# Softmax over slots by two pairs of chunks in the first batch, with a newly searched order of all work

## The chip, the cores and the metric

One core of one Trainium2 chip runs the whole kernel. The metric is device time in microseconds (us), the median of several executions. The engines are TensorE (PE in the rows; its weight loads are PEld), VectorE (DVE), ScalarE (ACT), GpSimd (POOL) and SyncE (SP), whose queue issues nearly all transfers.

## The reference

`x` is 4 batches of 12800 rows of 128 channels; `inducing` is 32 slots of 128. Attention runs twice, then a gated convolution of 5 taps:

```python
def mab(q, kv):
    s = scale * (q @ kv.transpose(0, 2, 1))
    s = s - s.max(-1, keepdims=True)
    a = np.exp(s)
    a /= a.sum(-1, keepdims=True) + 1e-09
    return a @ kv
h = mab(I, x)
x = mab(x, h)
...
for k in range(K):
    gate_pre += conv_w[k][None, None, :] * xp[:, k:k + S, :]
gate = 1.0 / (1.0 + np.exp(-gate_pre))
val = x @ w_val
return (gate * val @ w_out)
```

So the first attention reads all rows of a batch into 32 slots (h), and the second gives each row a softmax over those 32 slots.

## The kernel before

A batch's 12800 rows are four strips of 3200, one for each quarter of the partitions, and the strips are cut into seven chunks of 320 to 480 columns (`SIZES`). In the first batch the order of chunks starts with 1; chunk 0 is last.

For each batch there are two passes. In the first, `s1` (L313) multiplies a chunk of x with the inducing rows; `e1` (L318, VectorE) takes the scores from PSUM and keeps a maximum; `group` makes the negated maximum (L350, L352) on GpSimd or VectorE; `exp1` takes exponentials (L360) and transposes them (L363); `hsum` (L377) sums exp times x into H, which VectorE adds up (L389 to L393). In the first batch most of the transposed x is made by TensorE (L287) and copied out of PSUM (L293 on ScalarE, L295 on VectorE) and not loaded. `prep` turns H into the slots hT (L413, then L420 to L422) and into the convolution's weights W (L481, L490) from `w_val`, `w_out` and `conv_w`, which come as 64-bit numbers in one load (L163) and are converted by VectorE (L176 to L181), then by GpSimd (L192 to L201) or VectorE (L189 to L198); `wts` (L208 to L210) takes three small statistics of them. The slots need `wts` only for what follows them.

In the second pass `s2` (L530) scores a chunk against the slots, `tin` (L534, VectorE) transposes the scores out of PSUM into a tile e, and `joint` does the softmax for a list of chunks at once: maximum (L544, VectorE), subtraction (L549, GpSimd), exponential (L555, ScalarE), sum and reciprocal (L561, L563, L564, VectorE), product (L572, GpSimd), transpose back (L575, VectorE), the high half in f16 (L578, ScalarE) and the low half (L580, GpSimd). `JOINT` lists which chunks go together. A `visit` is the convolution of a chunk (L597 for the gate, L604 for the value); it needs the halves of its own chunk and of the one before. Then come tanh (L695, ScalarE), gate times value (L705, VectorE), two f16 halves (L712 ScalarE, L715 GpSimd), the output product (L786, TensorE), its copy out of PSUM (L798 VectorE or L800 ScalarE) and the store (L804).

Every engine works through its own queue in order. What stands in it is set by three tables: `ORDER` is the order in which all operations are issued, `SLOTS` gives each tile its buffer (PSUM has eight banks, and a product waits until the bank's last reader is done), and `ENGINES` chooses between two engines where an operation allows it. Transfers go in SyncE's queue in the same order.

Of the kernel before, what the change touches and what calls it, by code (L numbers as in the profile page):

```python
# [42 lines left out]
JOINT = [[[0], [1], [2], [3], [4], [5, 6]]] + [[[0], [1, 2], [3, 4], [5, 6]]] * 3  # L43
# [820 lines left out]
def run_plan(tc, plan, slot):  # L864
# [109 lines left out]
]  # L974
ENGINES = [
# [3 lines left out]
]  # L979
# [54 lines left out]
```

## Time and profile before

| | us |
|---|---|
| median of 3 runs | 269.8 (269.4 to 270.52) |
| the profiled execution | 270.69 |
| its span in the profile | 268.6 |
| TensorE busy | 261.0 (97%) |
| VectorE busy | 216.3 (81%) |
| GpSimd busy | 206.1 (77%) |
| ScalarE busy | 195.3 (73%) |

Busy times are shares of the span. TensorE's matmuls are pipelined, so a busy TensorE can hold short stalls that don't show as idle time. The profiled execution lies 0.9 us above the median.

### The profile page before, as it was taken

What the parts mean: (1) busy time and instruction counts of PE and PEld (TensorE: products, weight loads), DVE (VectorE), ACT (ScalarE), POOL (GpSimd) and SP (SyncE); (2) the same over time, 40 slices, a digit from 0 to 9 for tenths busy, and PEclk for the clock granted to TensorE, in tenths of its full rate; (3) what the DMA queues carried; (4) which work ended last, traced back from release to release, by engine and by line L of the source; (5) the groups of instructions that cost most, each with busy time, mean ns of one, the idle gap of its engine ahead of it and who ended that gap; (6) DMA issues with size and microseconds to landing.
All of it is one profiled execution on the core that took longest, in us unless ns stands there. A gap on an engine that the chain in (4) does not pass through costs nothing.

```text
span 268.6 us, 10638 instructions
## 1 busy us (share of the span) xinstructions
PE 261.0 (97%) x4609; PEld 142.1 (53%) x4609; DVE 216.3 (81%) x431; ACT 195.3 (73%) x247; POOL 206.1 (77%) x191
## 2 busy tenths in 40 slices
PE   8999899999999999999999999999999999999994
PEld 4658444476444457464444456457545655444442
DVE  0698799999888998979997888967899897783623
ACT  2466147896667788758778796897679898689674
POOL 1225277798979698886998888988889979989650
PEclk9999999999999999999999999999999999999999
DMA  7999999959999398999869999931550313634486
GB/s 264 424 418 420 414 420 385 355 201 418 343 418 380 115 333 296 357 335 367 316 228 361 350 301 311 399 139 53 198 205 4 142 68 144 223 144 155 156 302 226
DMA packets 22943, 74.48 MB, mean 277 GB/s; under 512 B 1905, under 2 KB 16241, under 8 KB 22897
## 3 DMA queue, kind: packets, MB, share of 16 engines
q1 hardware_dynamic: 22608, 73.61, 72.9%
q8 instruction: 36, 0.59, 0.9%
q10 hardware_dynamic: 288, 0.20, 0.2%
q14 instruction: 11, 0.08, 0.1%
HBM read 47.58 MB, written 26.21 MB: 275 GB/s over the span
## 4 chain that ended last, share of the span: by engine, by line
PE 82%; DMA 7%; DVE 6%; issue 2%; POOL 2%; ACT 1%; DVEq 0%; ACTq 0%
PE banks L597 31%; PE banks L786 23%; PE banks L377 8%; PE banks L530 7%; DMA os<-in_xt_dram 5%; PE banks L604 5%; PE banks L313 4%; DMA indT<-in_indT_dram 1%; PE banks L287 1%; PE banks L741 1%; DVE os L798 1%; PE banks L481 1%; DVE ss L318 1%; DVE z L561 1%; DVE m L544 1%
## 5 line engine op out<-in xcount | busy, mean ns | idle before, releaser
L715 POOL TENSOR_TENSOR gl<-tg,gh 128x960 f16<-128x960 f32 (+2 forms) x54 | 104.6, 1948 | 9.8 <-ACT gh L712 4.2
L597 PE MATMUL banks<-P,W 32*128 32x480 f16 (+3 forms) x1680 | 103.3, 351 | 0.3 <-POOL P L580 0.2
L705 DVE SCALAR_TENSOR_TENSOR tg<-tg,banks 128x960 f32<-128x960 f32 (+4 forms) x57 | 61.4, 1081 | 22.4 <-ACT tg L695 18.9
L597 PEld LDWEIGHTS <-W 32*128 32x128 f16 x1680 | 51.2, 92 | 45.4 <-issue 14.3
L695 ACT ACTIVATE tg<-banks,gsc 128x960 f32<-128x960 f32 (+4 forms) x57 | 55.0, 1007 | 15.8 <-PE banks L597 15.5
L712 ACT CAST gh<-tg 128x960 f16<-128x960 f32 (+2 forms) x54 | 51.5, 960 | 18.3 <-DVE tg L705 10.3
L786 PE MATMUL banks<-gh,wo 128*32 128x480 f16 (+4 forms) x636 | 64.1, 358 | 0.6 <-issue 0.6
L786 PEld LDWEIGHTS <-wo 128*32 128x32 f16 (+1 forms) x954 | 36.0, 97 | 34.9 <-issue 13.7
L786 PE MATMUL banks<-gl,wo 128*32 128x480 f16 (+4 forms) x318 | 43.5, 357 | 0.0
L604 PE MATMUL banks<-P,W 32*128 32x480 f16 (+3 forms) x336 | 41.4, 353 | 0.3 <-DVE ss L318 0.3
L800 ACT ACTIVATE os<-banks,osc 128x960 f32<-128x960 f32 (+2 forms) x33 | 33.8, 1031 | 8.1 <-PE banks L786 8.1
L580 POOL TENSOR_TENSOR P<-pt,P 128x480 f16<-128x480 f32 (+4 forms) x18 | 28.1, 1558 | 3.2 <-ACT P L578 3.0
L572 POOL TENSOR_TENSOR e<-e,z 128x480 f32<-128x480 f32 (+4 forms) x18 | 25.2, 1400 | 6.0 <-DVE z L564 5.5
L377 PE MATMUL banks<-xk,et 128*32 128x129 f32 x800 | 29.5, 275 | 0.2 <-ACT tg L695 0.2
L549 POOL TENSOR_TENSOR e<-e,m 128x480 f32<-128x480 f32 (+4 forms) x18 | 25.1, 1398 | 4.2 <-DVE m L544 4.1
L377 PEld LDWEIGHTS banks<-xk,et 128*32 128x32 f32 x800 | 24.6, 109 | 6.4 <-issue 2.1
L798 DVE TENSOR_SCALAR os<-banks,osc 128x960 f32<-128x960 f32 (+2 forms) x21 | 24.4, 1171 | 2.7 <-PE banks L786 2.6
L530 PE MATMUL banks<-xt,hT 128*32 128x480 f32 (+2 forms) x208 | 25.5, 557 | 0.0
L313 PE MATMUL banks<-xt,indT 128*32 128x480 f32 (+2 forms) x208 | 24.3, 554 | 0.0
L360 ACT ACTIVATE ss<-ss,ng 128x480 f32<-128x480 f32 (+3 forms) x28 | 17.3, 668 | 4.8 <-POOL ng L352 2.5
L534 DVE STREAM_TRANSPOSE e<-banks 128x480 f32<-128x480 f32 (+2 forms) x28 | 18.1, 654 | 1.2 <-PE banks L530 0.5
L363 DVE STREAM_TRANSPOSE et<-ss 128x480 f32<-128x480 f32 (+3 forms) x28 | 17.2, 636 | 1.7 <-ACT ss L360 1.7
(104 smaller groups left out, 263.2 us busy)
## 6 DMA issues: line engine op xcount, KB each, us to landing
xt<-in_xt_dram SPq DMA_DIRECT2D x16, 960.0 KB, 8.6
out_dram<-os SPq DMA_DIRECT2D x30, 480.0 KB, 4.4
xk<-in_xk_dram SPq DMA_DIRECT2D x11, 904.0 KB, 9.2
out_dram<-os SPq DMA_DIRECT2D x22, 448.0 KB, 3.9
xk<-in_xk_dram SPq DMA_DIRECT2D x10, 968.0 KB, 7.9
xt<-in_xt_dram SPq DMA_DIRECT2D x8, 896.0 KB, 11.9
os<-in_xt_dram SPq DMA_DIRECT2D x1, 960.0 KB, 14.6
xk<-in_xk_dram SPq DMA_DIRECT2D x1, 712.0 KB, 9.2
```

Of the source, the lines that this page charges most:

```text
L313: T.matmul(buf(key)[32 * r:32 * r + 32, :n], c_["indT"], x[:, :, r, :], start=True, stop=True)
L377: T.matmul(buf(key)[32 * s:32 * s + 32, :P + 1], buf(("et", b, c))[:, 32 * i:32 * i + 32], buf(("xk", b, c))[:, i, :], start=j < R, stop=j ...
L530: T.matmul(buf(key)[32 * r:32 * r + 32, :n], buf(("hT", b)), x[:, :, r, :], start=True, stop=True)
L580: lambda: G.tensor_tensor(c_["P2"][:, o:o + n], buf(qk)[:, :n], c_["P1"][:, o:o + n], ALU.subtract), ("lo", n),
L597: T.matmul(buf(("ps2", "g", b, c, r // 2))[:, r % 2, :n], buf(("W", b))[q, w, k, :], c_[("P1", "P2")[e]][q, o:o + n], start=u == 0, stop=u ...
L604: T.matmul(buf(("ps2", "v", b, c, r // 2))[:, r % 2, :n], buf(("W", b))[q, w, TAPS, :], c_[("P1", "P2")[e]][q, o:o + n], start=u == 0, sto ...
L695: lambda s=s: S.activation(buf(tg)[:, s, :n], buf(g)[:, s, :n], AF.Tanh, scale=small[b]["gsc"]),
L705: V.scalar_tensor_tensor(t, t, 1.0, buf(v)[:, s, :n], ALU.add, ALU.mult)
L712: op(("hi", b, c, p), "ACT", lambda: S.copy(buf(g1)[:, :, :n], buf(tg)[:, :, :n]), ("act", 2 * n), [("gv", b, c, p, 0)], [g1], [tg])
L715: ENG[e].tensor_tensor(buf(g2)[:, :, :n], buf(tg)[:, :, :n], buf(g1)[:, :, :n], ALU.subtract)
L786: T.matmul(t[s], w[:, s], x, start=j == 0, stop=j == len(terms) - 1)
L800: S.activation(o, a, AF.Copy, scale=small[b]["osc"])
```

## The change

In the first batch the softmax over slots was done for chunks 1, 2, 3 and 4 alone and for 5 with 6. Now it is done for 1 alone, 2 with 3, 4 with 5, and 6 alone. There is one softmax group fewer, 1178 operations in place of 1186. The three tables are new throughout, for all batches.

```diff
-JOINT = [[[0], [1], [2], [3], [4], [5, 6]]] + [[[0], [1, 2], [3, 4], [5, 6]]] * 3
+JOINT = [[[0], [1], [2, 3], [4, 5], [6]]] + [[[0], [1, 2], [3, 4], [5, 6]]] * 3
...
 ORDER = [
-    1, 0, 2, 15, 13, 16, 17, 18, 19, 3, 20, 21, 14, 28, 27, 47, 123, 125, 30, 29, 129, 55, 126, 31, 124, 132,
+    1, 0, 2, 15, 13, 16, 17, 18, 19, 20, 21, 14, 3, 28, 27, 47, 124, 123, 55, 29, 126, 125, 30, 56, 130, 129,
```

First place: SyncE's queue at the start of the program. xt and os are chunks of x, tg is the tile that takes the weights (w), xk a chunk of transposed x.

```order
 L257 DMA xt_64<-in_xt_dram 128x1920
 L257 DMA xt_65<-in_xt_dram 128x1920
-L163 DMA tg_83<-in_w_dram 128x261
 L257 DMA xt_66<-in_xt_dram 128x1920
 L257 DMA os<-in_xt_dram 128x1920
 L257 DMA os<-in_xt_dram 128x1408
+L163 DMA tg_83<-in_w_dram 128x261
 L257 DMA xk_114<-in_xk_dram 128x1936
```

The load of the weights went behind the three loads of chunks 5, 6 and 0.

Second place: VectorE before the slots hT, in the program before. ss and et are a chunk's scores and their transposed exponentials, H the sum, w the converted weights, cmax and wrow what `wts` makes.

```order
L363 STREAM_TRANSPOSE et1_78<-ss4_76 128x480
L335 TENSOR_REDUCE m10_130<-mx0_129 128x1
L363 STREAM_TRANSPOSE et2_79<-ss0_72 128x480
L295 COPY xk0_113<-banks_61 128x7x128
L208 TENSOR_REDUCE cmax_127<-w_123 128x1
L209 TENSOR_SCALAR cmax_127<-cmax_127 128x1
L210 TENSOR_REDUCE wrow_128<-w_123 128x1
L363 STREAM_TRANSPOSE et0_77<-ss1_73 128x320
L391 SCALAR_TENSOR_TENSOR H0_94<-H0_94,f0_133,banks_61 128x129 x2
L420 TENSOR_SCALAR zz0_134<-banks_61 128x32
```

The same stretch of VectorE's queue in the changed program, from the sixth maximum of the batch on:

```order
L335 TENSOR_REDUCE m10_130<-mx0_129 128x1
L176 TENSOR_SCALAR tg1_84<-tg0_83 128x261
L177 SCALAR_TENSOR_TENSOR tg1_84<-tg0_83,tg1_84 128x261
L391 SCALAR_TENSOR_TENSOR H0_94<-H0_94,f0_133,banks_61 128x129
L178 SCALAR_TENSOR_TENSOR tg1_84<-tg0_83,tg1_84 128x261
L318 TENSOR_SCALAR ss1_73,mx0_129<-banks_61 128x320
L179 TENSOR_SCALAR tg1_84<-tg1_84 128x261
...
L189 SCALAR_TENSOR_TENSOR tg2_85<-tg2_85,tg1_84 128x261
L190 TENSOR_TENSOR tg2_85<-tg2_85,tg1_84 128x261
L181 TENSOR_SCALAR tg0_83<-tg0_83 128x261
L391 SCALAR_TENSOR_TENSOR H0_94<-H0_94,f0_133,banks_61 128x129
L198 SCALAR_TENSOR_TENSOR w_123<-tg0_83,tg2_85 128x261
```

The whole conversion now stands among the last steps to H; its last three instructions (L189, L190, L198) were on GpSimd before, and its first (L176) stood some 15 rows further up.

Third place: TensorE's queue from the slots to the first convolution, before. os holds chunks 0 and 6 of the first batch, xt0 to xt4 chunks 1 to 5, xt5 to xt9 chunks of the second batch. The lines left out make W (L481).

```order
L530 MATMUL banks_61<-os_117,hT0_111 32x352 x4
L451 MATMUL banks_61<-hT0_111,w_123 32x32 x4
L530 MATMUL banks_61<-xt0_62,hT0_111 32x480 x4
L530 MATMUL banks_61<-xt2_64,hT0_111 32x480 x4
...
L313 MATMUL banks_61<-xt7_69,indT_121 32x480 x4
L313 MATMUL banks_61<-xt8_70,indT_121 32x448 x4
L313 MATMUL banks_61<-xt9_71,indT_121 32x448 x4
L313 MATMUL banks_61<-xt6_68,indT_121 32x448 x4
```

And in the changed program:

```order
L530 MATMUL banks_61<-os_117,hT0_111 32x352 x4
L451 MATMUL banks_61<-hT0_111,w_123 32x32 x4
L530 MATMUL banks_61<-xt0_62,hT0_111 32x480 x4
L530 MATMUL banks_61<-os_117,hT0_111 32x480 x4
L313 MATMUL banks_61<-xt7_69,indT_121 32x448 x4
...
L313 MATMUL banks_61<-xt5_67,indT_121 32x448 x4
L530 MATMUL banks_61<-xt2_64,hT0_111 32x480 x4
L530 MATMUL banks_61<-xt1_63,hT0_111 32x480 x4
L313 MATMUL banks_61<-xt8_70,indT_121 32x448 x4
...
L530 MATMUL banks_61<-xt3_65,hT0_111 32x480 x4
```

Six slot-score products (L530) stand ahead of the first convolution where three stood, and three scores of the second batch (L313) where four stood.

## Rows read from the trace of the kernel before

**Rows 1.** Stretches: us, busy us of each engine (x instructions), clock, DMA, GB/s

```profile
21.20:30.10 8.90, 8.26 (x169) 6.09 (x158) 6.61 (x22) 4.29 (x8) 3.19 (x9) 1.00 1.01 418
30.10:37.50 7.40, 6.79 (x116) 2.27 (x117) 6.99 (x27) 3.20 (x6) 4.80 (x10) 1.00 1.02 419
37.50:51.20 13.70, 13.04 (x253) 6.76 (x253) 13.38 (x37) 8.22 (x14) 10.86 (x18) 1.00 0.98 380
...
63.80:100.00 36.20, 36.13 (x656) 16.95 (x656) 32.48 (x59) 27.68 (x34) 31.95 (x26) 1.00 0.89 329
100.00:150.00 50.00, 50.00 (x973) 27.53 (x966) 43.62 (x93) 38.31 (x49) 42.87 (x35) 1.00 0.90 322
150.00:200.00 50.00, 49.43 (x1035) 27.97 (x1027) 41.72 (x78) 39.36 (x50) 43.34 (x35) 1.00 0.68 244
...
sum 268.60, PE 261.04 PEld 142.05 DVE 216.29 ACT 195.30 POOL 206.14; mean PE 26.10 PEld 14.21 DVE 21.63 ACT 19.53 POOL 20.61
```

**Rows 2.** Timeline of TensorE: start, us, line, [idle before <-releaser]

```profile
14.29 1.93 PE L377 MATMUL banks<-xk,et 128*32 128x129 f32 x60
...
28.88 0.33 PE L413 MATMUL banks<-pick,H 128*32 128x32 f32 x16 [0.51 <-DVE H L391]
...
30.14 0.80 PE L530 MATMUL banks<-os,hT 128*32 128x352 f32 x8 [0.18 <-DVE hT L422]
...
30.82 1.80 PE L530 MATMUL banks<-xt,hT 128*32 128x480 f32 x16
...
37.48 1.54 PE L597 MATMUL banks<-P,W 32*128 32x320 f16 x40
39.27 0.86 PE L597 MATMUL banks<-P,W 32*128 32x320 f16 x18 [0.24 <-POOL P L580]
...
63.82 0.37 PE L597 MATMUL banks<-P,W 32*128 32x480 f16 x2
...
67.81 0.96 PE L530 MATMUL banks<-xt,hT 128*32 128x448 f32 x8
68.58 0.59 PE L786 MATMUL banks<-gh,wo 128*32 128x480 f16 x8
...
69.19 0.59 PE L786 MATMUL banks<-gh,wo 128*32 128x480 f16 x8
```

**Rows 3.** Groups by line and shape, to 75 us: count, busy us, mean ns

```profile
L575 DVE STREAM_TRANSPOSE pt<-e 128x480 f32<-128x480 f32 x4 | 2.7, 672 | 0.0
...
L544 DVE TENSOR_REDUCE m<-e 128x15 f32<-128x480 f32 x4 | 2.5, 632 | 0.0
...
L575 DVE STREAM_TRANSPOSE pt<-e 128x960 f32<-128x960 f32 x1 | 1.2, 1172 | 0.0
...
L544 DVE TENSOR_REDUCE m<-e 128x30 f32<-128x960 f32 x1 | 1.1, 1146 | 0.0
```

**Rows 4.** Timeline of SyncE's queue, then transfers: KB each, us to landing

```profile
3.15 0.45 SPq L163 DMA_DIRECT2D tg<-in_w_dram  x1
...
4.71 0.81 SPq L257 DMA_DIRECT2D os<-in_xt_dram  x2
...
os<-in_xt_dram SPq DMA_DIRECT2D x1, 704.0 KB, 16.0
...
tg<-in_w_dram SPq DMA_DIRECT2D x1, 261.0 KB, 10.1
```

**Rows 5.** Timeline of VectorE, 15 to 31 us: start, us

```profile
15.22 0.29 DVE L176 TENSOR_SCALAR tg<-tg 128x261 int32<-128x261 int32 x1
...
15.55 0.43 DVE L177 SCALAR_TENSOR_TENSOR tg<-tg,tg 128x261 int32<-128x261 int32 x1
...
21.58 0.85 DVE L352 TENSOR_SCALAR ng<-n 32x1 f32<-32x1 f32 x4
...
29.28 0.19 DVE L420 TENSOR_SCALAR zz<-banks 128x32 f32<-128x32 f32 x1 [0.46 <-PE banks L413]
...
29.90 0.19 DVE L422 TENSOR_TENSOR hT<-banks,zz 128x32 f32<-128x32 f32 x1
```

158 rows, old and new, of tables (ENGINES, ORDER, SLOTS) are left out of this document.

## The prediction

> **What bounds the kernel now.** I read a table of stretches, then TensorE's timeline. In the table [rows 1] the reader is to see two regimes. From 63.8 us on TensorE is busy for 36.13 of 36.20 us and 50.00 of 50.00, at a granted clock of 1.00, and over the whole span for 261.04 of 268.60: there nothing can be won but TensorE's own work. That work does not change. Both programs have 32 runs of convolution matmuls with 33 runs of other matmuls between them, and the same products in sum; the after has a few more output products in one piece and fewer in strips, at the same number of columns.
>
> What is left to decide is the first 64 us, where TensorE has waits and VectorE is nearly full: 6.61 of 8.90 us before the slots hT exist, then 6.99 of 7.40 and 13.38 of 13.70 [rows 1]. In TensorE's timeline [rows 2] the landmarks are: the H matmuls at 28.88 after 0.51 idle, the first slot scores (L530) at 30.14, the first convolution at 37.48, and the convolution of chunk 3, the fourth visit, at 63.82. I measure the change by how much TensorE has done when it reaches that last landmark.
>
> **The pairing itself.** Four single chunks and a pair become two singles and two pairs: 1 and 6 alone, 2 with 3, 4 with 5. That is one softmax group fewer, and with it five VectorE, three GpSimd and two ScalarE instructions fewer. On VectorE two maxima of 480 cost 2 x 0.632 us and one of 960 costs 1.146; two transposes cost 2 x 0.672 against 1.172 [rows 3]. That saves 0.118 and 0.172; the sum, the scaling and the reciprocal, which I take at 0.12 each, make it 0.65 us of VectorE. It is worth 0 if TensorE has other work meanwhile, and 0.65 if VectorE is what TensorE waits for. Against it stands latency: chunk 2 now waits for chunk 3 in every step, each longer by some 0.5 us (1.146 - 0.632).
>
> By the rows the part that an instruction costs whatever its width is 2 x 0.632 - 1.146 = 0.118 us. [...]
>
> **The weights' conversion, moved.** On SyncE's queue the load of the weights (tg from w) went from before the load of chunk 5 to behind the last x load of the batch. It was issued at 3.15 and landed 10.1 us later, at 13.25; the last x load (os, 704 KB), the second of the two issued from 4.71 on, took 16.0 and landed at about 21.1 [rows 4]. With the same bytes ahead, the weights now land about when that load did, 21.1, and the x loads land earlier by 261 KB at 418 GB/s [rows 1], 0.6 us. In VectorE's order the first conversion (L176) stands behind chunk 6's maximum and ahead of chunk 0's, so it holds that queue until the weights are there. From 21.2 on VectorE then has three things to do before hT. First the six conversions, which ran in its gaps from 15.22 on before: two of them took 0.29 and 0.43 [rows 5], 1.9 in all. Second, three instructions of the same width that GpSimd did before: 3 x 0.43 = 1.3. Third the stretch's own work: 6.61 us busy [rows 1], less 1.1 for the group's negated maximum (L350 and L352, which goes to GpSimd), less 0.8 for hT itself, plus 0.3 for a small copy that ScalarE did: 5.0. Together 8.2, so that hT starts at 29.4, against 29.28 before [rows 5]: **+0.1 us**. What hid the conversion before were gaps, 2.3 us in this stretch alone (8.90 - 6.61); that cover is used up. If the weights land later, every microsecond goes onto hT in full; hT can be earlier by 0.4 at most, by the x load. Upper bound 1.7: the loads issued behind the weights share the engines.
>
> **From hT to the second visit.** I count VectorE's queue at 0.6 us for each 448- or 480-wide instruction, 1.15 for a 960-wide one [rows 3], and estimate 0.5 for a 352-wide and 0.2 for a small one (hT's last took 0.19 [rows 5]); used on the old order this gives 0.6 too much over 7.4 us, so I scale by 0.92. The first visit needs four banks, the last of them freed by chunk 2's slot transpose: 8 wide, 4 narrow and 13 small instructions behind hT, 9.4 x 0.92 = 8.7, so at about 39.0. That is 1.5 us after 37.48. But TensorE has more to do until then: six slot-score products for three, and three batch-1 scores for four, +2 x 0.8 (two products took 1.6 [rows 2]). Cost about 0. The second visit needs a bank that chunk 5's maximum of batch 1 frees, nine VectorE rows on (five wide, one pair, three small): 4.5 us, 43.5. TensorE is there at 39.0 + 2.3 (visit 0 without its idle time [rows 2]) + 1.6 (two scores) = 42.9, so it waits 0.6; before, it waited 0.24 for GpSimd's low half in the first visit [rows 2]. **+0.3 us.**
>
> **The first pair.** VectorE ends the pair's last transpose 16 rows on, 8.3 us: 51.8; ScalarE's copy of 960 takes about 1.0, so the third visit can start at 52.8. TensorE comes there at 43.5 + 4.0 (visit 1, as the fourth took from 63.82 to 67.81) + 3 x 0.95 (three h sums; two took 1.9 at 14.29) + 1.6 + 0.6 + 0.9 = 53.5 [rows 2]: no wait, with 0.7 of cover. If the cover is gone, chunks 2 and 3 are late together. Then come 4.4 us of visit, four h sums (3.8) and two outputs (0.9): 62.6. The last h sum waits for a transpose behind ten more us of VectorE, at 62.0, so the fourth visit starts at about 63.0. Before it started at 63.82, but with two output products (0.6 each, as L786 at 68.58 and 69.19 [rows 2]) and 0.2 of H matmuls already done: 62.4 in the same coin. **+0.6 us in all**, the 0.1 and 0.3 included.
>
> **The rest.** From there on no wait was left to lose, and in the last 40 TensorE operations only the turn of some outputs differs: 0.0, between -0.6 (the idle time of 150 to 200 [rows 1]) and +1.0 (as much again as the early waits cost).
>
> **The sum.** The profiled execution took 270.69 us (span 268.6 and 2.1 around it), 0.9 above the median of 269.8. 270.69 + 0.6 = 271.3; less 0.9, **270.4 us** as a median.
>
> **The rivals.**
> 1. No change to speak of (my forecast): the waits move, TensorE's work is the same. Own range 269.0 to 271.1. Chance 0.55.
> 2. Slower, by one mechanism: the weights' load. Its place is VectorE's first conversion behind chunk 6's maximum. It decides from a landing at 21.9 us on, 0.7 later than I took, for 0.6 + 0.8 is 1.4 over before. At the upper bound, 22.8, hT is 1.7 late and the time is 270.4 + 1.7 = 272.1. For it: loads of this stretch took up to 16.0. Against it: the bytes ahead are the same. Chance 0.2.
> 3. Slower: the pair is late at the third visit, whose cover is 0.7. If VectorE or GpSimd are 1.7 later than I counted, 1.0 is lost: 271.4. Chance 0.08.
> 4. Faster: VectorE's 0.65 us come through, and half of TensorE's waits from 21.2 to 51.2 go (0.64 + 0.61 + 0.66 = 1.9 us [rows 1]): 269.8 - 0.65 - 0.95 = 268.2. For it: VectorE is 98% busy from 37.5 to 51.2. Against it: I find the banks freed late in the new queue. Chance 0.17. [...]
>
> **Numbers.** 0.5% of 269.8 is 1.35 us, about what a measurement tells from no change. Faster by more than that 0.17, same 0.55, slower 0.28 (rivals 2 and 3). The range reaches into rivals 2 and 4 until a fifth is left out: 268.7 to 272.3.
>
> **What would show it.** Right: the weights land near 21 us; hT (L422) at 29.9 to 30.3; first convolution near 39.0, second visit near 43.5 after a wait of some 0.5 for VectorE's L318 or L534, third near 53.5, fourth near 63.0; no idle time of TensorE after 65 us. Wrong: a conversion held until 22 with hT after 30.7; idle time over 0.5 us after 65 us beyond what was there; a third visit that waits for ScalarE's P copy (L578); or a first convolution before 38.0, which would mean that banks came free earlier than I counted.

## The result: slower by 0.85%, and not in the head

The changed kernel takes 271.85 us (median of 17 runs, 270.61 to 274.93), the kernel before 269.8 in the same comparison (268.62 to 270.66): a ratio of 1.0085 with a 95% interval of 1.0065 to 1.0104. That is beyond the 0.5% that the prediction took for the limit of a measurement. The ratios in this document compare fast executions alone (of the 17 the one of 274.93 us is slow) and are not quotients of the medians. The prediction's 270.4 is 1.45 us short of it; its range, 268.7 to 272.3, holds it. The profiled execution took 271.85 us with a span of 269.9.

The stretches of the changed kernel, in the columns of [rows 1]:

```profile
21.20:30.10 8.90, 8.10 (x159) 5.94 (x155) 8.38 (x28) 3.91 (x7) 3.04 (x11) 1.00 1.01 419
30.10:37.50 7.40, 7.26 (x124) 2.62 (x120) 7.08 (x26) 2.12 (x5) 4.08 (x7) 1.00 1.02 418
37.50:51.20 13.70, 13.35 (x262) 8.13 (x256) 13.08 (x31) 10.63 (x17) 10.99 (x19) 1.00 0.88 335
63.80:100.00 36.20, 36.20 (x624) 18.20 (x616) 32.91 (x67) 29.26 (x36) 32.52 (x27) 1.00 0.91 332
100.00:150.00 50.00, 48.70 (x1004) 27.50 (x1000) 44.28 (x84) 35.61 (x45) 41.77 (x32) 1.00 0.87 310
150.00:200.00 50.00, 48.74 (x984) 29.29 (x980) 42.32 (x89) 38.81 (x48) 40.33 (x31) 1.00 0.69 251
```

The reader is to compare TensorE's busy time, the first figure behind the comma. From the slots hT on the head is fuller than in [rows 1] (7.26 for 6.79, 13.35 for 13.04). From 100 to 200 us, where TensorE had idled for 0.57 us, it now idles for 1.30 + 1.26 = 2.56 us. ScalarE and GpSimd are less busy there than before (74.4 us for 77.7, 82.1 for 86.2), VectorE a little busier (86.6 for 85.3).

TensorE's timeline, in the columns of [rows 2], tells where:

```profile
28.52 0.33 PE L413 MATMUL banks<-pick,H 128*32 128x32 f32 x16 [0.46 <-DVE H L391]
29.79 0.80 PE L530 MATMUL banks<-os,hT 128*32 128x352 f32 x8 [0.18 <-DVE hT L422]
38.08 0.31 PE L597 MATMUL banks<-P,W 32*128 32x320 f16 x3
38.63 1.14 PE L597 MATMUL banks<-P,W 32*128 32x320 f16 x28 [0.24 <-DVE m L335]
42.40 0.81 PE L597 MATMUL banks<-P,W 32*128 32x480 f16 x6
52.07 0.38 PE L597 MATMUL banks<-P,W 32*128 32x480 f16 x2
61.39 0.38 PE L597 MATMUL banks<-P,W 32*128 32x480 f16 x2
116.07 0.44 PE L377 MATMUL banks<-xk,et 128*32 128x129 f32 x7 [0.24 <-issue]
122.63 0.37 PE L597 MATMUL banks<-P,W 32*128 32x448 f16 x4 [1.05 <-issue]
183.82 0.42 PE L377 MATMUL banks<-xk,et 128*32 128x129 f32 x8 [1.17 <-issue]
```

The visits begin at 38.08, 42.40, 52.07 and 61.39, the second, third and fourth without a wait. By the prediction's coin (62.4 for the kernel before) the fourth is 1.0 us early. Then come three waits, 2.46 us together, that the profile puts down to "issue": no semaphore, no transfer, no other engine. All three stand in the middle of a stream of matmuls for which the profile shows nothing else to wait for. The kernel before had one such wait over 0.1 us after 40 us:

```profile
169.68 0.54 PE L786 MATMUL banks<-gh,wo 128*32 128x448 f16 x5 [0.57 <-issue]
```

The steps of the head in detail. VectorE's groups to 75 us, as in [rows 3]:

```profile
L575 DVE STREAM_TRANSPOSE pt<-e 128x960 f32<-128x960 f32 x2 | 2.3, 1172 | 0.3 <-POOL e L572 0.3
L544 DVE TENSOR_REDUCE m<-e 128x30 f32<-128x960 f32 x2 | 2.2, 1111 | 0.0
L544 DVE TENSOR_REDUCE m<-e 128x15 f32<-128x480 f32 x3 | 1.9, 636 | 0.0
```

The pairs are there, at the prices that the prediction took. The weights' load and its landing, as in [rows 4]: the issue in SyncE's timeline, then the transfer.

```profile
4.92 0.44 SPq L163 DMA_DIRECT2D tg<-in_w_dram  x1
```

```profile
tg<-in_w_dram SPq DMA_DIRECT2D x1, 261.0 KB, 16.0
```

It landed at 4.92 + 16.0 = 20.9, and VectorE's timeline, as in [rows 5], has the conversion right there and hT 0.36 us earlier than before:

```profile
20.95 0.30 DVE L176 TENSOR_SCALAR tg<-tg 128x261 int32<-128x261 int32 x1
...
29.54 0.19 DVE L422 TENSOR_TENSOR hT<-banks,zz 128x32 f32<-128x32 f32 x1
```

### What the waits have in common

I counted TensorE's records (matmuls, weight loads and the few others of its queue) from the start of each trace up to the first record behind a wait for "issue", which is not counted itself:

```
kernel    wait ends at   line   count   remainder over 256
before        169.68     L786    6081   193
after         116.07     L377    4033   193
after         122.63     L597    4289   193
after         183.82     L377    6593   193
```

Four of four stand at the same place of a block of 256. (The expectations below say 193 or 194, since some of their counts take in the record itself.) The profile's list of DMA queues has a queue for instructions, and 35 packets of it in the changed kernel, 0.57 MB: 16 KB each, one for every 256 of TensorE's 9132 records.

```profile
q8 instruction: 35, 0.57, 0.9%
```

Two windows of the DMA queues (packets, MB, share of 16 engines) show the second wait. TensorE took up a block's first instruction at 116.07; in the next 4.2 us no instruction packet moved, while the data queue was full:

```profile
q1 hardware_dynamic: 343, 1.65, 101.3%
```

and in 120.3 to 121.4, after it, the packet came:

```profile
q1 hardware_dynamic: 187, 0.41, 98.6%
q8 instruction: 1, 0.02, 5.5%
```

It ended at 121.31, and TensorE went on at 122.63. The same for other blocks of this trace, from the records of queue 8; lag is the time from the first use of the block before to the start of the packet:

```
first use of the block before   lag    packet ends   next block's first use
103.62                          1.39   106.31        109.23
109.23                          4.44   114.62        116.07  (waited 0.24)
116.07                          4.29   121.31        122.63  (waited 1.05)
176.74                          4.73   182.41        183.82  (waited 1.17)
195.40                          0.18   196.71        202.85
```

In this trace a block's packet starts at the earliest 0.8 us ahead of the first use of the block before it (202.85). Where the data queue has room (a DMA share of 0.55 from 195 to 202 us) it starts 0.2 us behind that use, in the full stretches up to 4.7 us behind it; it mostly takes 1.0 us, and in no trace of this document was a block used sooner than 1.2 us behind its packet. TensorE uses up a block in 6.6 us on average (43.8 to 202.8 us), so that by an estimate from these figures a lag over some 4.3 us (6.6 - 1.0 - 1.3) is a wait, and a smaller one where the block's instructions are short. The waits at these blocks are of 0.24 to 1.17 us in this trace, and of 0.17 (run 4) to 1.55 us (run 12) over all runs. That TensorE waits there for blocks which a full data queue held up is the **fetch theory**. Its rivals: the **order theory**, that the new order has a dependency at these places that the profile doesn't show, and the **pairing theory**, that the loss comes from the first batch's softmax.

### The profile page after: what moved, and what is told of

It reads as the page before. It is cut to its first block, busy times and chain, and to the rows that moved or that the text cites. A ratio compares the mean times of both kernels' runs of the same rounds, so it can differ in the third digit from the quotient of the medians.

```text
span 269.9 us, 10489 instructions
## 1 busy us (share of the span) xinstructions
PE 261.4 (97%) x4543; PEld 146.2 (54%) x4543; DVE 221.3 (82%) x445; ACT 193.3 (72%) x241; POOL 198.2 (73%) x171
## 3 DMA queue, kind: packets, MB, share of 16 engines
q1 hardware_dynamic: 22608, 73.61, 73.1%
## 4 chain that ended last, share of the span: by engine, by line
PE 83%; DVE 10%; issue 2%; POOL 2%; ACT 1%; POOLq 0%; ACTq 0%
PE banks L597 29%; PE banks L786 23%; PE banks L377 8%; PE banks L530 6%; PE banks L604 6%; PE banks L313 6%; PE banks L287 3%; DVE ss L318 1%; PE banks L216 1%; DVE tg L705 1%; DVE et L363 1%; PE banks L741 1%; ACT tg L695 1%; PE banks L481 1%; DVE e L534 1%
## 5 line engine op out<-in xcount | busy, mean ns | idle before, releaser
L597 PEld LDWEIGHTS <-W 32*128 32x128 f16 x1680 | 53.5, 92 | 43.9 <-issue 16.1
L786 PE MATMUL banks<-gh,wo 128*32 128x448 f16 (+4 forms) x600 | 63.8, 357 | 0.0
L786 PEld LDWEIGHTS <-wo 128*32 128x32 f16 (+1 forms) x900 | 36.8, 97 | 32.2 <-issue 11.0
L786 PE MATMUL banks<-gl,wo 128*32 128x448 f16 (+4 forms) x300 | 44.4, 356 | 0.0
L377 PE MATMUL banks<-xk,et 128*32 128x129 f32 x800 | 29.5, 275 | 1.6 <-issue 1.4
L377 PEld LDWEIGHTS banks<-xk,et 128*32 128x32 f32 x800 | 24.6, 109 | 8.4 <-issue 4.6
L572 POOL TENSOR_TENSOR e<-e,z 128x960 f32<-128x960 f32 (+4 forms) x17 | 25.0, 1471 | 4.5 <-DVE z L564 2.4
L580 POOL TENSOR_TENSOR P<-pt,P 128x960 f16<-128x960 f32 (+4 forms) x17 | 27.8, 1636 | 0.5 <-ACT P L578 0.3
L798 DVE TENSOR_SCALAR os<-banks,osc 128x960 f32<-128x960 f32 (+1 forms) x21 | 24.6, 1178 | 3.0 <-PE banks L786 2.9
L549 POOL TENSOR_TENSOR e<-e,m 128x960 f32<-128x960 f32 (+4 forms) x17 | 24.9, 1471 | 1.6 <-DVE m L544 1.5
L313 PE MATMUL banks<-xt,indT 128*32 128x480 f32 (+2 forms) x208 | 25.5, 558 | 0.1
L530 PE MATMUL banks<-xt,hT 128*32 128x480 f32 (+2 forms) x208 | 24.7, 557 | 0.1
L318 DVE TENSOR_SCALAR_CACHE_REDUCE ss<-banks 128x480 f32<-128x480 f32 (+3 forms) x28 | 17.3, 619 | 1.4 <-PE banks L313 1.1
L578 ACT CAST P<-pt 128x960 f16<-128x960 f32 (+4 forms) x17 | 14.0, 826 | 5.6 <-DVE pt L575 5.6
```

Of the source, the lines that this page charges most:

```text
L313: T.matmul(buf(key)[32 * r:32 * r + 32, :n], c_["indT"], x[:, :, r, :], start=True, stop=True)
L377: T.matmul(buf(key)[32 * s:32 * s + 32, :P + 1], buf(("et", b, c))[:, 32 * i:32 * i + 32], buf(("xk", b, c))[:, i, :], start=j < R, stop=j ...
L530: T.matmul(buf(key)[32 * r:32 * r + 32, :n], buf(("hT", b)), x[:, :, r, :], start=True, stop=True)
L580: lambda: G.tensor_tensor(c_["P2"][:, o:o + n], buf(qk)[:, :n], c_["P1"][:, o:o + n], ALU.subtract), ("lo", n),
L597: T.matmul(buf(("ps2", "g", b, c, r // 2))[:, r % 2, :n], buf(("W", b))[q, w, k, :], c_[("P1", "P2")[e]][q, o:o + n], start=u == 0, stop=u ...
L786: T.matmul(t[s], w[:, s], x, start=j == 0, stop=j == len(terms) - 1)
```

## The experiments

Times are medians of the kernel's own comparison, beside the kernel before on the same chip: 270.12 (runs 1 to 4), 269.7 (5 to 8), 269.78 (9 to 11), 269.68 (12). Behind a median stand its ratio to the kernel before and the 95% interval. What is read of waits and blocks is read from one profiled execution of each.

**1. TensorE's stream shifted by 128.**

```diff
-        for _ in range(WARM):
-            T.matmul(buf(("ps", "warm")), c_["zero"][:, :P], c_["zero"], start=True, stop=True)
+        for _ in range(72):
+            T.matmul(buf(("ps", "warm"))[:, :56], c_["zero"][:, :P], c_["zero"][:, :56], start=True, stop=True)
```

> The changed kernel, with the eight warm-up matmuls of 512 columns at TensorE's start written as 72 of 56 columns: nearly the same columns, but every later TensorE instruction stands 128 places further on in the stream (a matmul and its weight load are two). Three theories for the waits of TensorE that the profile of the changed kernel puts down to nothing (0.24, 1.05 and 1.17 us; 0.57 in the kernel before). Fetch theory: TensorE's instructions come in 16 KB blocks over a DMA queue of their own, and a block that is asked for while the data queue is full comes late; counted in the trace from the start, all four waits end on an instruction whose count leaves 193 or 194 over a multiple of 256. Then the waits stand here at other instructions of the program, their counts again leave about 193, and the time moves within 269.5 to 273. Order theory: the newly searched order holds a dependency there that the profile does not show; then they stay at the same instructions of the program (the gate products of the visit that began at 118.7 and the H product at 183.8), and the time stays 271.9 within 0.5. Pairing theory (the loss sits in the first batch's softmax): no statement on these waits, 271.9 within 0.5.

Measured: 271.4 us (1.0041, 1.0020 to 1.0062). No wait for "issue" over 0.1 us is left after 40 us, though every operation and its order is the same. The stretches 100 to 150 and 150 to 200:

```profile
100.00:150.00 50.00, 49.95 (x1028) 28.12 (x1020) 45.58 (x87) 37.05 (x45) 41.72 (x33) 1.00 0.90 323
150.00:200.00 50.00, 49.91 (x1012) 29.04 (x1004) 43.79 (x92) 39.28 (x49) 41.83 (x31) 1.00 0.72 260
```

That speaks against the order theory: the same instructions no longer wait. By itself it doesn't settle it, for the head of this profile is late and everything behind it meets the transfers at another time: TensorE's first work waited 0.62 and 0.77 us for loads, and hT came at 31.27, not 29.54. Runs 6 and 7 settle it. The late head is also why the time fell by 0.45 us only.

**2. Small stores.**

```diff
-            nc.sync.dma_start(out[b, :, 2 * p + q:2 * p + q + m, FIRST[b][c]:FIRST[b][c] + n], buf(os)[:, q:q + m, :n])
+            k = n if b > 2 else 32
+            nc.sync.dma_start(out[b, :, 2 * p + q:2 * p + q + m, FIRST[b][c]:FIRST[b][c] + k], buf(os)[:, q:q + m, :k])
```

> The changed kernel, where each output store of the first three batches writes 32 of its columns and not 320 to 480 (most of the output is not written): a third of the bytes in the middle of the span are gone, no instruction of TensorE moves. Fetch theory: the block requests find a less full data queue, at most one wait over 0.3 us put down to nothing is left, time 269.0 to 270.0 (1.9 to 2.9 below the changed kernel). Order theory: the same waits at the same places, 271.9 within 0.5. Pairing theory: 271.9 within 0.5.

Measured: 269.38 us (0.9981, 0.9961 to 1.0001), 2.5 below the changed kernel; no wait for "issue" is left.

```profile
100.00:150.00 50.00, 49.85 (x1032) 28.02 (x1024) 45.54 (x90) 36.97 (x46) 42.61 (x32) 1.00 0.61 213
150.00:200.00 50.00, 49.91 (x1004) 29.20 (x992) 43.69 (x90) 39.65 (x50) 41.51 (x32) 1.00 0.39 132
```

TensorE's instructions and their counts are unchanged, and so is the number of data packets (22608); the bytes fell (73.6 MB to 55.3), the DMA share with them (0.87 to 0.61, 0.69 to 0.39), and the waits went. The median lag of a block (begun between 40 and 210 us) fell from 1.80 to 0.71 us, the largest from 4.73 to 3.82.

**3. All output products in one piece.**

```diff
-            forms[j] = "strips" if strips else "full"
+            forms[j] = "full"
```

> The changed kernel, with each output product as three matmuls of 128x128 weights everywhere, not as twelve of 128x32 in 64 of 113 cases: the same columns, about 1150 TensorE instructions fewer, and changes between the two tile forms of TensorE where there were none. Fetch theory: a block of 256 instructions lasts longer, so the same lateness of a block is covered: no wait over 0.3 us put down to nothing, which gives 2 us back; what the changes of tile form cost, no row shows, so the time is 269.5 plus that cost. Order theory: the waits stay, time 271.9 plus that cost. Pairing theory: the same as order theory.

Measured: 274.36 us (1.0157, 1.0127 to 1.0188). With 7908 records in place of 9132 (and 31 instruction packets, not 35) a block lasts 8.2 us on average, not 6.6, and no wait for "issue" is left, as the fetch theory has it. But from the fourth visit to the end this execution took 210.1 us, where the changed kernel's second profile (run 8) takes 206.0 without its waits: the changes of tile form cost about 4.1 us over 64 products. It is no remedy. Its hT came at 32.1; its first transposes and first products with the inducing rows were slow (1.83 us for eight L313 where run 8 shows 1.01), at a granted clock of 1.00 from 4 to 12 us, which I leave open.

**4. The pair of chunks 2 and 3 undone.** Its core; `new` names a buffer as new for the first chunk and as used for the second, and `h`, `l` are the chunk's place in the shared buffers, which stand in every instruction of the group.

```diff
-            joint(b, cs)
+            for own in [[q] for q in cs] if (b, cs) == (0, [2, 3]) else [cs]:
+                joint(b, own, cs[0])
...
+        l = sum(wid(b, c) for c in range(first, cs[0]))
+        h = l // 32
+        ek, mk, zk, qk = [(s, b, first) for s in ("e", "m2", "z", "pt")]
...
-            e = buf(ek)[:, :nb]
+            e = buf(ek)[:, h:h + nb]
```

> The changed kernel with the pair of chunks 2 and 3 of the first batch undone: each chunk has its own maximum, subtraction, exponential, sum, product and copies again, in the changed kernel's order, side by side, in the same buffers. Pairing theory in the form of the prediction (pairing saves VectorE's fixed costs, 0.65 us, and gives less than that on TensorE; the head's place is set by the order): the fourth visit begins at 61.4 within 0.4, the time is that of the changed kernel within 0.5. If the pair itself made the head earlier by 1.0 us (fourth visit at 61.4 where 62.4 answers to the kernel before), it begins at 62.2 to 62.8 here and the time is 0.5 to 1.2 longer. Fetch theory: no TensorE instruction moves in the stream, so the waits stay on the same counts, though they may grow or shrink with the time at which the loads stand.

Measured: 271.94 us (1.0059, 1.0038 to 1.0081), the changed kernel's time. The fourth visit began at 62.17, but hT came later too, at 30.27: from hT to the fourth visit it is 31.90 us here and 31.85 in the changed kernel. Both stretches, with VectorE as the third engine, in the changed kernel and then here:

```profile
29.54:61.39 31.85, 31.18 (x623) 18.09 (x620) 30.67 (x79) 21.64 (x33) 22.73 (x29) 1.00 0.91 341
```

```profile
30.27:62.17 31.90, 31.20 (x622) 17.84 (x618) 30.98 (x84) 21.85 (x35) 23.14 (x32) 1.00 0.89 338
```

Five instructions of VectorE more, and 30.98 against 30.67: the pair does save VectorE 0.31 us of busy time (0.69 as the sum of its instructions' own times, for records that follow one another overlap, as in the changed kernel L178, from 22.05 to 22.49, and L318, from 22.41), and it is worth nothing in time. The three waits are back on the same counts, 0.17, 0.78 and 1.42 us. The pairing theory is out for chunks 2 and 3; the pair of 4 and 5 stood, and its undoing was not tried.

**5. The kernel before with the same small stores** (the edit of 2).

> The kernel before, with each output store of the first three batches writing 32 of its columns (most of the output is not written), as was done to the changed kernel, which came to 269.4 that way. With few bytes in the way neither kernel should wait for instructions, so the two small-store kernels compare the two orders without that term. Fetch theory: the kernel before loses its one wait of 0.57, so 269.3 to 269.9, and the two small-store kernels agree within 0.5: all of the difference between the kernels was late instruction blocks. If the new order's head is really 1.0 us ahead, as the two single profiles showed, this kernel comes to 270.0 to 270.8. Order theory (the new order's steady part is worse by about 2 us for reasons other than the blocks): 267.0 to 268.0 here, 2 below the changed kernel with the same stores.

Measured: 269.56 us (0.9993, 0.9975 to 1.0010). With small stores the two orders are 269.38 and 269.56, 0.2 apart (0.3 by their ratios, 0.9981 and 0.9993, whose intervals overlap); with whole stores they are 2.05 and 1.7 apart in two comparisons. TensorE idles for nothing from 100 to 200 us:

```profile
100.00:150.00 50.00, 50.00 (x970) 27.48 (x962) 43.35 (x93) 38.18 (x47) 42.67 (x37) 1.00 0.58 202
150.00:200.00 50.00, 50.00 (x1036) 28.11 (x1028) 42.43 (x82) 40.37 (x51) 43.96 (x35) 1.00 0.38 124
```

Both other outcomes that were named, 270.0 to 270.8 and 267.0 to 268.0, lie outside the interval (0.9975 to 1.0010 of 269.7 is 269.0 to 270.0), the first of them only just.

**6 and 7. A shift by 64, of the changed kernel and of the kernel before.** The same edit for both:

```diff
             T.matmul(buf(("ps", "warm")), c_["zero"][:, :P], c_["zero"], start=True, stop=True)
+        for _ in range(32):
+            T.matmul(buf(("ps", "warm"))[:, :56], c_["zero"][:, :P], c_["zero"][:, :56], start=True, stop=True)
```

> The changed kernel with 32 matmuls of 56 columns behind the eight warm-up matmuls, in the 2.7 us that TensorE idles there before the first chunk: every later instruction stands 64 places further on. Fetch theory: waits that the profile puts down to nothing, if there are any, end on counts that leave about 193 over a multiple of 256, so at instructions of the program 64 places before those of the changed kernel; time 269.4 to 273, by how many blocks come late. Order theory: the old three places, 271.9 within 0.5. A second question is the head: in the 128-place shift the first chunk's work waited 1.4 us for the loads and the first convolution began at 39.8 (38.1 in the changed kernel's profile). If that was chance of one execution, the first convolution is at 38.0 to 38.8 here.

> The kernel before with the same 32 short matmuls, 64 places of shift. Fetch theory: the one wait of 0.57 leaves its place, and others may come where a block is used up in under 5.5 us with the data queue full, on counts that leave about 193: time 269 to 272, not bound to 270.1. Order theory: the kernel before has a better order, whose waits do not depend on where blocks begin: 270.1 within 0.4, its 0.57 at the same instruction.

Measured: 270.8 (1.0040, 1.0015 to 1.0066) and 270.4 us (1.0034, 1.0015 to 1.0054): the old order gets worse by it, and the new one better (1.0040 for the 1.0083 of run 8, with intervals that overlap). The changed kernel's waits, TensorE's timeline (two lines of code more, so L379 is L377 and L788 is L786):

```profile
61.09 1.52 PE L379 MATMUL banks<-xk,et 128*32 128x129 f32 x43 [0.74 <-issue]
...
68.75 0.38 PE L788 MATMUL banks<-gl,wo 128*32 128x480 f16 x3 [1.00 <-issue]
...
123.26 0.56 PE L599 MATMUL banks<-P,W 32*128 32x448 f16 x8 [0.60 <-issue]
...
188.10 0.54 PE L788 MATMUL banks<-gh,wo 128*32 128x448 f16 x5 [0.51 <-issue]
```

The counts are 1985, 2241, 4289 and 6849, each with the remainder 193; at the old instructions of the program (4353 and 6657 in the shifted count) nothing waits. The profiled execution is the slowest of its runs, 273.17. In the kernel before the wait is again on count 6081, and so at another instruction, an H product where it was an output product:

```profile
169.07 0.49 PE L379 MATMUL banks<-xk,et 128*32 128x129 f32 x9 [0.80 <-issue]
```

The order theory's words for run 7 (270.1 within 0.4, the wait at the same instruction) hold the time but not the place. TensorE has no 2.7 us of idle time behind its warm-up, as I had written for run 6: with the eight alone the first transposes start at 4.56. They started 0.9 later here, and hT still came at 29.98.

**8. The changed kernel again** (no edit).

> The changed kernel itself, beside the others on one chip. Fetch theory: the waits end on the same counts (4033, 4289, 6593) when they come, with other sizes (their lateness depends on what the data queue holds), time 271.3 to 272.4. A second profile also shows how far the head's place (first convolution at 38.1 in the first) belongs to the kernel or to one execution: if it is the kernel's, 38.1 within 0.3; if not, anywhere from 38 to 40.

Measured: 271.41 us (1.0083, 1.0051 to 1.0115). The waits end on the counts 4289 and 6593 again:

```profile
122.68 0.37 PE L597 MATMUL banks<-P,W 32*128 32x448 f16 x4 [1.05 <-issue]
...
183.37 0.42 PE L377 MATMUL banks<-xk,et 128*32 128x129 f32 x8 [0.69 <-issue]
```

hT came at 29.81, the first convolution at 38.34, the fourth visit at 61.64, 0.25 later than in the first profile. From hT to the fourth visit it is 31.83 us, as in the first (31.85): that step belongs to the kernel, while hT itself varies from one execution to the next.

**9 and 10. Packets of half the size**, in the changed kernel and in the one before; with the layout of the loads in memory following the constant.

```diff
-PARTS = 1
+PARTS = 2
```

> The changed kernel with each partition's row of a load in two pieces, so that a load's packets are of about 3.8 KB and not 7.7 KB (the same bytes, the same loads). The fetch theory stands; the question is what a late block waits behind. If it waits behind a number of packets (depth theory), its lag behind the previous block's end, 4.3 to 4.7 us at the three late blocks, falls to some 2 to 3 us, no wait put down to nothing is left, and the time is 269.3 to 270.3: a version that loses nothing to the kernel before. If it waits behind a number of bytes, or until the loads have come in (bytes theory), the lags and the three waits stay and the time is 271.3 to 272. If small packets move fewer bytes a second, the first convolution, at 38.1 and 38.3 in two profiles, is later than 38.6.

> The kernel before with the same packets of half the size. Depth theory: its one late block is in time, 269.0 to 269.5. Bytes theory: 269.8 within 0.3 with its 0.57 wait. Slower loads would show as a later first convolution and 270 or more.

Measured: 270.93 (1.0044, 1.0021 to 1.0067) and 270.24 us (1.0012, 0.9992 to 1.0033). The lags of the three late blocks fell by 6 to 20%, to 4.17, 3.81 and 3.78 us, not by half. In run 8, without an edit, they were 4.26, 4.05 and 4.17, so that of the fall 2 to 9% is left. Two of the three waits are left:

```profile
122.38 0.37 PE L597 MATMUL banks<-P,W 32*128 32x448 f16 x4 [0.78 <-issue]
...
182.68 0.42 PE L377 MATMUL banks<-xk,et 128*32 128x129 f32 x8 [0.28 <-issue]
```

That is neither outcome clean; the depth theory's numbers are missed. The loads were slower too: the first convolution came at 38.61, and 407 GB/s moved from 6 to 30 us where runs 5 to 8 had 420. In the kernel before no visible wait is left, and nothing is gained.

**11. The 128 once more, with another warm-up**: the edit of 6 with `range(5)` for the eight and `range(67)` for the 32.

> The changed kernel shifted by 128 places once more, now with five warm-up matmuls of 512 columns and 67 of 56, to keep TensorE busy about as long as the eight did. The first 128-place shift had no wait put down to nothing, but 271.4 us and its first chunk waited 1.4 us for loads. If that lateness was chance of one execution or came of its warm-up, hT is at 29.5 to 30.3 here, no block is late, and the time is 269.2 to 270.2. If blocks were late in its other executions after all, the time is again 270.8 to 271.8, whatever this profile shows.

Measured: 271.7 us (1.0065, 1.0045 to 1.0084). The warm-up ran longer than meant (the first transposes start at 6.43, not 4.56), hT came at 31.0, and one block was late:

```profile
67.25 0.58 PE L599 MATMUL banks<-P,W 32*128 32x480 f16 x8 [0.96 <-issue]
```

In run 1 this very block was just in time (used 1.35 us behind its packet), so that run 1's other executions may well have had waits that its profile doesn't show. What part of the two 128-place times is the late head and what part late blocks is not separated.

**12. Loads of half the size**, each as two DMAs.

```diff
-TRANSFERS = 1
+TRANSFERS = 2
```

> The changed kernel with each load issued as two DMAs of half the bytes (rows of about 3.8 KB, one DMA behind the other on the same queue), and so twice as many issues on SyncE. Smaller packets alone brought the lags of the three late blocks from 4.44, 4.29 and 4.73 us to 4.17, 3.81 and 3.78. Unit theory: a block waits until the engine that carries it has done its share of the DMAs in hand; a 960 KB load is 8 rows on each of 16 engines, 8 x 0.29 = 2.3 us (a packet of 7680 bytes took some 0.29), so the largest lags are two such shares. With half loads they fall to about 2.4, no wait put down to nothing is left, and the time is 269.4 to 270.4, if the added issues on SyncE (0.4 us each) cost the head nothing. Bytes theory: the engine's backlog is what counts, whatever its units; lags of 3.8 to 4.2 as with the smaller packets, one to three waits, 270.6 to 271.5.

Measured: 271.88 us (1.0080, 1.0057 to 1.0102); the profiled execution is the slowest of its six, 273.77. The lags grew, to 5.11 and 4.87 at the first two late blocks; the second wait is the longest of all runs:

```profile
125.69 0.55 PE L597 MATMUL banks<-P,W 32*128 32x448 f16 x7 [1.55 <-issue]
```

The unit theory falls, and the head paid for the added issues (hT at 31.72). Its 8 rows on each engine were an estimate, a load's 128 packets shared evenly by 16 engines; the trace doesn't show which engine carries a packet. What a block waits behind stays open. Runs 9 and 12 divided the loads alone; the stores' packets (480 columns of 4 bytes, under 2 KB) stayed as they were, and in the 1.1 us in which the second late block came, 120.3 to 121.4, 176 of 188 packets were under 2 KB. Nor does the number of packets set the lag, for run 2 had as many and its median lag fell to 0.71.

**All runs by one count**: blocks (of those after 40 us) that were used at most 1.55 us behind their packet's end, that is, just when they came, in the one profiled execution; the visible waits for "issue" of that execution; and the median.

```
kernel                        just-in-time blocks   waits, us   median, us
2   after, small stores               0               0.0        269.38
5   before, small stores              0               0.0        269.56
    before                            1               0.57       269.8
10  before, half packets              1               0.0        270.24
7   before, shift 64                  5               0.80       270.4
6   after, shift 64                   6               2.85       270.8
9   after, half packets               4               1.06       270.93
1   after, shift 128                  4               0.0        271.4
8   after, again                      4               1.74       271.41
11  after, shift 128, warm            3               0.96       271.7
    after                             4               2.46       271.85
12  after, half loads                 3               2.23       271.88
4   after, unpaired                   5               2.37       271.94
3   after, all in one piece           0               0.0        274.36
```

The limit of 1.55 was chosen after the runs, and runs 2, 7, 9 and 11 have blocks at 1.58 to 1.66 us that it leaves out. Kernels with no more than one such block take 269.4 to 270.2 (run 3 apart, which pays 4 us for its tile forms), kernels with three or more 270.4 to 271.9; among these the number of blocks doesn't order the times. All 19 visible waits of the table end on a count with the remainder 193. No version of the new order with whole stores comes down to the kernel before.

## Why the prediction was right or wrong

- The range held the result by luck: its upper end, 272.3, reached into rival 2, a late landing of the weights, which didn't happen. Two terms of the sum were wrong, and with opposite signs. By its own sign the prediction was wrong too: TensorE's idle time from 100 to 200 us rose from 0.57 to 2.56 us, where over 0.5 more after 65 us was to show it.
- **The rest** is the step that failed: "From there on no wait was left to lose", with 0.0 us between -0.6 and +1.0. From the fourth visit to the end the changed kernel's profile has 208.5 us and the one before 204.8, and 1.4 of the difference is work that stood ahead of the fourth visit before: 2.3 us, beyond the term's upper bound, of which 2.46 - 0.57 = 1.9 are late instruction blocks. The wait of 0.57 us was in the trace of before, ending 169.68 us into it; I used it as the lower bound of the term and did not ask what it waited for. Runs 5 and 7 showed that it was a late instruction block: it went with small stores, and with a shift of 64 places it came on the same count at another instruction. The remaining 0.4 us I have not traced; in the small-store pair, without late blocks, it is 0.3 (205.6 - 203.9 - 1.4), of which 0.24 is idle time of TensorE from 100 to 200 us.
- **hT, +0.1 us**: measured -0.36 and -0.09 in the two profiles of the changed kernel. The landing was forecast at 21.1 and came at 20.9. Over all profiles with the usual warm-up and loads, run 3 apart, hT is at 29.3 to 29.9 with the old order and 29.5 to 30.3 with the new; the term is right within that scatter.
- **From hT to the fourth visit**: with the steps at 39.0, 43.5, 53.5 and 63.0 I forecast a loss of 0.5 us behind hT (0.6 less hT's 0.1). Measured are 38.08, 42.40, 52.07 and 61.39. The old order takes 33.9 us from hT to the fourth visit in four profiles, 32.5 in the coin without the 1.4; the new one takes 31.8 to 31.9 in every profile (in run 6 less the 0.74 of a late block), with the pair or without. So the step is worth -0.65 us, where +0.5 was forecast: the second wrong term. The landmarks came 0.9, 1.1, 1.4 and 1.6 us before the forecast, of which L422 at 29.54, forecast for 29.9 to 30.3, explains 0.4 to 0.8: my count of VectorE's queue put the freed banks too late by the rest, as I read it; the wait of 0.6 ahead of the second visit never came, and the 0.24 in the first visit stayed under another name (L335).
- **The pairing, 0.65 us of VectorE**: by run 4 it is 0.69 for one pair as a sum of instructions' own times, as the prediction worked it out, but 0.31 of busy time; and it was worth nothing in time, as one of its two bounds had it: TensorE had other work.
- **The rivals**: the late landing (2) didn't happen, nor the late pair (3): the third visit waits for nothing. Of the faster one (4) the half on TensorE came in part, about 1.0 us at the fourth visit in the first profile, but by the order and not the pair of chunks 2 and 3. The mechanism that decided the sign was none of the four. No change (1), given 0.55, was wrong by a measurable 0.85%.
- The sum in profiles: -1.0 to the fourth visit, +1.9 late blocks, +0.4 unexplained, +1.3; the spans differ by 269.9 - 268.6 = 1.3. The medians differ by 2.05 and 1.7, since the before's profiled execution was 0.9 above its median and the changed kernel's at its median. What made it slower isn't found; its hT, at 29.90, was 0.56 later than in run 5.

## What to carry to other kernels

A TensorE wait for "issue" in the middle of a stream of ready matmuls deserves a count: if its place is the same over 256 in several traces, an instruction block that came late is the first thing to look for, in the packets of the instruction queue. Here it appeared where short instructions (with 128x32 tiles a block lasted 6.6 us) met a full data queue (a DMA share of 0.87 from 100 to 150 us; with 0.61, in run 2, no wait was left). Two orders that differ by less than a per cent can then be told apart by no more than where the blocks happen to begin; leaving out transfers in both, or shifting the stream, separates that from what the orders themselves are worth. And an idle time in a stretch that is "full" should be explained before it is used as a bound.

## What was not expected of the hardware

- Data transfers hold up instruction blocks: with 55.3 MB of them in place of 73.6 (run 2) the median lag was 0.71 us and not 1.80. In the changed kernel a block's packet started within 0.8 us of the first use of the block before, on either side, after 195 us (DMA share 0.41 from 210 to 255), and up to 4.7 us behind it in full stretches (5.5 in run 7). But for one packet (2.7 us ahead, run 6) none started over 1.5 us ahead of that use, so that in these traces a block came about one block ahead of TensorE.
- A shift of one engine's stream by 64 places, with the operations behind it unchanged, moved the medians by 0.6 (271.41 to 270.8) and 0.7 us (269.7 to 270.4), in opposite directions for the two orders; only the second is clear of noise.
- Smaller packets of the loads, and smaller DMAs, did little for the lag (4.17, 3.81 and 3.78 us in run 9, for 4.26, 4.05 and 4.17 in run 8) or raised it (5.11 and 4.87 in run 12).
